# A transformer block with hedgehog linear attention: feature-map weights as one block spread by one-hot products, load waits as own queue entries, new orders of loads and queues

## The chip, the cores and the metric

The kernel runs on one core of one Trainium2 chip. The metric is the time of one execution in device microseconds (us). The profile is of one execution, taken by the hardware profiler.

## The reference, cut to what matters

One block on 2048 tokens of width 448, in bf16: a layer norm, linear attention with 16 heads of 28, a residual, a second layer norm, a gated unit of width 1792, a residual.

```
xn  = layernorm(x)
q, k, v = split(xn @ wqkv)                     # 16 heads, Dh = 28
pq, pk  = q @ w_phi[h], k @ w_phi[h]           # w_phi: 16 x 28 x 28
phi(p)  = concat(softmax(p), softmax(-p))      # 56 features
kv, z   = phi_k^T v, sum_s phi_k
o       = (phi_q kv) / (phi_q z + 1e-6)
h   = x + o @ wo
out = h + (sigmoid(n(h) @ w_gate) * (n(h) @ w_up)) @ w_down     # n = layernorm
```

## The kernel before, in words

Every piece of work is an entry (`op`, lines 29 to 67) with a name, an engine, a function and the keys that it reads and writes. `ORDER` (lines 221 to 288) writes out by hand, for each of the five engines, the names in the order in which its queue has them. `emit` (lines 110 to 191) works out from the keys which semaphores an entry waits for, issues the waits in front of it (lines 177 to 181), and leaves out those that the engine is already known to have passed. Queues are in order: an entry that waits holds up everything behind it on its engine. `PROGRAM` (lines 290 to 295) lists the stages of the second half.

The 2048 tokens are 16 tiles of 128. The names, with t for the tile:

- Loads, on SP's queue: x tiles (`x0`, `x1`, then two at a time as `x2`, `x4` and so on, line 480), `ld_k*` and `ld_v*` (the k and v thirds of wqkv), `ld_q*` (the q third, transposed by the DMA, line 483), `ld_wo*`, `ld_wg*`, `ld_wu*`, `ld_wd*`. `xT4` to `xT15`, `oT*` and `hT*` from tile 2 on are DMA transposes on the same queue (lines 563, 803, 839).
- First layer norm: `bst`/`agg` on DVE (lines 525, 526), `pow1_*` on POOL (534), `nm1_*` (538), `xn` (550 to 556, on ACT, DVE or POOL as `ORDER` says). For tiles 0 to 3 `xT` is a PE transpose (518) and `xTe` its copy out of PSUM (511).
- The feature map is folded into the weights. `Wphi` is a block-diagonal matrix for four groups of four heads: zeroed by `bd0` (line 415), then filled by four DMAs on ACT's queue, `wphi0` to `wphi3` (line 476), in rows of 56 bytes. `wT0` to `wT3` transpose Wk on PE (579), `wTe` copies the result out, `w2m0_*` multiplies it by Wphi (592) and `w2e0_*` copies that to SBUF as the folded k weights. `w2m1_*` and `w2e1_*` (592, 609) do the same for q, from the `ld_q` transposes.
- Projections: `ppa`/`ppb` and `vva`/`vvb` for tiles 0 to 3 in pairs, `pva`/`pvb` from tile 4 on (lines 628 to 639, products at line 309); the first need the folded k weights and xT, `vva0` the v weights. Per tile then: `ek` (two exponentials on ACT, 651 and 652), `v1` (v copied out, 511), `ss` and `rs` (sums and reciprocals on DVE, 655 and 661), `phi` (product on POOL or DVE, 665), and `kva`/`kvb`, which add the tile to kv in PSUM.
- q features: `pqa`/`pqb`, then `eq` on ACT (701). `kvz*` copy kv out by parts (730, 734), with `kvzones` (456), `mask2` (448) and `par` (450) as small constants made from the identity `ident` (417). `num`, `rsm`, `qq`, `b`, `c`, `rden` and `o` (lines 756 to 793) form the attention output.
- `woa`/`wob` are the output projection (848 to 872), `bs2`, `h`, `hn`, `hT` the residual, norm and transpose; `ga`/`gb` are gate and up (877 to 890), `sig` and `hh` the gate (891, 892), `dn`, `dp`, `dm`, `dl` the down products, `fin` the last residual (926), `out` the store.

At the start PE runs products of zeros (`warm0` to `warm9`, line 504) between its entries: 9 of 512 columns, then 35 of 128. Any PE entry that reads `wo` weights lists four load keys, any gate/up entry eight; the waits stand at the first such entry, `woa0` and `ga0_1`.

Of the kernel before, what the change touches and what calls it, by code (L numbers as in the profile page):

```python
# [6 lines left out]
ALU = mybir.AluOpType  # L7
# [11 lines left out]
class Graph:  # L19
# [90 lines left out]
    def emit(self, nc):  # L110
# [50 lines left out]
        with ExitStack() as es:  # L161
            sems = {n: es.enter_context(nc.semaphore("s_%s_%s" % n)) for n in names}
            with nc.Block() as block:
                start = {"sp": block.sync, "act": block.scalar, "pe": block.tensor, "dve": block.vector,
                         "pool": block.gpsimd}
                for e in ENGINES:
# [3 lines left out]
                    def body(eng, q=queues[e], e=e):  # L170
                        seen = {}
                        for n, o in enumerate(q):
                            if e == "sp" and n == len(q) - 5:
                                for sem, v in last_out.items():
                                    if sem[0] != "out":
                                        eng.wait_ge(sems[sem], v)
                            for j in o.waits:
                                p = ops[j]
                                if seen.get(p.sem, 0) < p.val:
                                    seen[p.sem] = p.val  # L180
                                    eng.wait_ge(sems[p.sem], p.val)
                            ins = o.fn(eng)
                            if o.dma is not None:
                                ins.then_inc(sems[o.sem], 16)
                            elif o.need_inc:
                                ins.then_inc(sems[o.sem], 1)
# [10 lines left out]
DH = 28  # L197
# [25 lines left out]
        "x1 x0 ld_k0 x2 ld_k2 x4 x6 ld_v0 x10 ld_v2 x8 ld_q2 ld_q1 ld_q0 x12 ld_q3 xT4 xT5 x14 xT6 xT7 xT8 xT9 xT10 "  # L223
# [6 lines left out]
        "wphi3 wphi2 wphi1 wphi0 par wTe0 xT0e nm1_3 w2e0_0 w2e0_2 w2e0_1 xT3e nm1_2 nm1_4 ek1 ek0 v1_1 v1_0 nm1_8 "  # L230
        "kvzones nm1_6 xn6 ek2 v1_2 ek3 v1_3 ek4 v1_4 w2e1_1 ek5 w2e1_0 ek6 v1_6 w2e1_3 ek7 v1_7 nm1_12 ek8 v1_8 "
        "w2e1_2 v1_9 ek9 ek10 v1_10 ek11 v1_11 v1_12 ek12 eq0_0p ek13 eq0_0m ek14 v1_14 ek15 v1_15 eq0_1p eq0_1m "
        "eq1_0m kvzC kvzA eq1_0p eq1_1p eq1_1m eq2_0p eq2_0m oT1e eq2_1p eq2_1m h0 h1 eq3_0m eq3_0p eq3_1p eq3_1m "
        "sig0_1 sig0_0 sig0_3 sig0_2 sig0_5 sig0_4 sq2 sig0_7 sig0_6 sq3 sig0_9 sig0_8 sig0_11 sig0_10 sig0_12 "
        "sig0_13 sq5 sq7 sq4 sig2_0 sig2_1 sq6 sig2_2 sig2_3 sig2_5 sig2_4 sig2_6 sig2_7 sig2_8 sig2_9 sig2_10 "
        "sig2_11 sig2_12 sig2_13 sig4_1 sq9 sig4_0 sig4_3 sq8 sig4_2 sig4_5 sig4_4 sig4_7 sig4_6 sig4_9 sq10 sig4_8 "
        "sq11 sig4_11 sig4_10 sig4_13 sig4_12 sig8_1 sig8_0 sq13 sig8_2 sig8_3 sig8_4 sig8_5 sq12 sig8_6 sq14 sq15 "
        "sig8_7 sig8_9 sig8_8 sig8_10 sig8_11 sig8_13 sig8_12 sig12_0 sig12_1 sig12_3 sig12_2 sig12_5 sig12_4 sig12_7 "
        "sig12_6 sig12_9 sig12_8 sig12_11 sig12_10 sig12_12 sig12_13 "
    ),  # L240
    "pe": (
        "warm0 warm1 warm2 xT1 warm3 wT0 warm4 wT1 warm5 warm6 xT0 warm7 wT2 w2m0_0 wT3 w2m0_2 w2m0_1 w2m0_3 warm8 "
        "warm9 xT3 ppa0 ppb0 vva0 xT2 vvb0 ppa2 vva2 ppb2 seed vvb2 w2m1_0 w2m1_1 pva4 kva0 pvb4 pva5 kvb0 kva1 pvb5 "
        "pva6 kvb1 pvb6 pva7 kva2 w2m1_3 w2m1_2 pvb7 pva8 kvb2 kva3 pvb8 kvb3 kva4 pva9 kvb4 pvb9 pva10 pqa0_0 pvb10 "
        "kva5 pva11 kvb5 kva6 pvb11 pva12 kvb6 kva7 pvb12 kvb7 pqb0_0 kva8 pva13 kvb8 kva9 pvb13 pva14 kvb9 kva10 "
        "pvb14 pva15 kvb10 kva11 pvb15 pqa0_1 kvb11 kva12 pqb0_1 pqa1_0 kvb12 kva13 pqb1_0 kvb13 kva14 kvb14 kva15 "
        "kvb15 qs pqa1_1 num0 pqb1_1 num1 pqa2_0 num2 pqb2_0 pqa2_1 oT0 oT1 num3 pqb2_1 woa0 wob0 num4 pqa3_0 pqb3_0 "
        "pqa3_1 num5 pqb3_1 hT0 hT1 num6 ga0_1 ga0_0 gb0_1 gb0_0 woa2 num7 ga0_3 ga0_2 gb0_3 gb0_2 wob2 num8 ga0_5 "
        "ga0_4 gb0_5 gb0_4 woa4 ga0_7 ga0_6 gb0_7 gb0_6 wob4 num9 ga0_9 ga0_8 gb0_9 gb0_8 woa6 ga0_11 ga0_10 gb0_11 "
        "gb0_10 wob6 ga0_13 ga0_12 gb0_13 gb0_12 dn0_0 dn0_4 ga2_1 ga2_0 gb2_1 gb2_0 num10 dn0_8 dn0_11 ga2_2 ga2_3 "  # L250
        "gb2_2 gb2_3 dp0_0 ga2_4 ga2_5 gb2_4 gb2_5 dp0_4 dp0_8 dp0_11 ga2_6 ga2_7 gb2_6 gb2_7 woa8 ga2_8 ga2_9 gb2_8 "
        "gb2_9 wob8 num11 ga2_10 ga2_11 gb2_10 gb2_11 dn2_0 ga2_12 ga2_13 gb2_12 gb2_13 dn2_4 dn2_8 ga4_1 num12 gb4_1 "
        "ga4_0 dn2_11 gb4_0 dp2_0 ga4_3 ga4_2 gb4_3 dp2_4 num13 gb4_2 ga4_5 dp2_8 gb4_5 ga4_4 dp2_11 gb4_4 ga4_7 "
        "num14 gb4_7 ga4_6 woa10 gb4_6 ga4_9 wob10 gb4_9 ga4_8 num15 gb4_8 ga4_11 woa12 gb4_11 ga4_10 wob12 gb4_10 "
        "ga4_13 dn4_0 ga4_12 gb4_13 gb4_12 dn4_4 ga8_1 ga8_0 gb8_1 gb8_0 dn4_8 dn4_11 ga8_3 ga8_2 dp4_0 gb8_2 dp4_4 "
        "dp4_8 gb8_3 ga8_4 dp4_11 gb8_4 ga8_5 woa14 gb8_5 ga8_6 wob14 gb8_6 ga8_7 dn6_0 gb8_7 dn6_4 ga8_8 ga8_9 dn6_8 "
        "gb8_9 gb8_8 dn10_0 dn6_11 ga8_11 ga8_10 gb8_11 gb8_10 dp6_0 dp6_4 dp6_8 ga8_13 ga8_12 gb8_13 gb8_12 dp6_11 "
        "dn10_4 dn10_8 ga12_0 ga12_1 gb12_0 dn8_0 dn10_11 gb12_1 ga12_2 dp10_0 ga12_3 dn8_4 dn8_8 gb12_3 gb12_2 "
        "dn8_11 dp10_4 ga12_5 dp8_0 ga12_4 gb12_5 gb12_4 dp8_4 dp8_8 ga12_7 ga12_6 gb12_7 gb12_6 dp10_8 dp10_11 "
        "dp8_11 ga12_9 ga12_8 gb12_9 gb12_8 dm14_0 dm14_4 dm13_0 dm14_8 dm12_0 dm13_4 ga12_11 ga12_10 gb12_11 gb12_10 "  # L260
        "dm15_0 dm15_4 dm13_8 ga12_12 ga12_13 gb12_12 gb12_13 dm14_10 dm12_4 dm13_10 dm12_8 dm13_12 dm13_13 dm12_10 "
        "dm14_12 dm12_12 dm12_13 dm15_8 dm14_13 dm15_10 dm15_12 dm15_13 dl15_0 dl15_12 "
    ),
    "dve": (
        "zero bd0 mask2 bst1 agg1 bst0 agg0 xn1 xT1e xn0 wTe1 bst3 bst2 agg3 wTe2 agg2 wTe3 bst4 w2e0_3 bst5 bst7 "
        "bst10 agg5 agg4 bst8 bst11 bst6 agg8 xT2e agg6 agg7 bst9 agg10 agg11 agg9 ss0 ss1 rs0 bst13 phi0 rs1 bst12 "
        "ss2 bst15 rs2 ss3 v1_5 bst14 ss4 agg14 rs3 rs4 agg13 agg12 phi3 agg15 ss5 ss6 rs5 rs6 phi5 ss7 rs7 phi6 ss8 "
        "rs8 xn14 ss9 ss10 rs9 rs10 phi9 ss11 rs11 v1_13 ss12 rs12 ss13 rs13 ss14 ss15 rs14 rs15 phi14 phi15 kvzD "
        "kvzB rsm0 qq0 b0 c0 b1 rden0 c1 rsm2 rden1 qq2 b2 c2 oT0e rsm3 qq3 b3 rden2 c3 o2 rden3 bs2_1 rsm4 bs2_0 qq4 "
        "ag2_1 ag2_0 b4 c4 hn1 hn0 rsm5 qq5 b5 hT0e c5 hT1e rden4 rsm6 rden5 qq6 b6 c6 hh0_1 rden6 hh0_0 rsm7 qq7 b7 "  # L270
        "c7 hh0_3 hh0_2 h3 h2 rden7 rsm8 qq8 hh0_5 hh0_4 b8 ve2 c8 hh0_7 hh0_6 h4 h5 hh0_9 hh0_8 hh0_11 hh0_10 h7 h6 "
        "rsm9 hh0_12 hh0_13 qq9 b9 ve5 c9 ve7 hh2_0 rden8 rsm10 hh2_1 qq10 ve6 o8 b10 hh2_2 nm4 hh2_3 rden9 nm5 o9 "
        "c10 hh2_4 hh2_5 fin1 fin0 hh2_6 hh2_7 hh2_8 hh2_9 h9 h8 hn7 rden10 hh2_10 hh2_11 rsm11 qq11 nm9 b11 hh2_13 "
        "c11 hh2_12 rsm12 qq12 nm8 b12 c12 rden11 hh4_1 hh4_0 o10 hh4_3 rsm13 qq13 b13 rden12 hh4_2 c13 hh4_5 fin3 "
        "hn9 rden13 hh4_4 hn8 fin2 rsm14 hh4_7 o13 qq14 b14 c14 hh4_6 h10 h11 nm10 hh4_9 nm11 rsm15 hn10 hh4_8 hn11 "
        "hh4_11 qq15 h13 h12 hh4_10 b15 c15 hh4_13 nm13 hh4_12 nm12 rden15 o15 rden14 hh8_1 hh8_0 o14 hh8_2 hh8_3 "
        "fin4 fin5 hh8_4 hh8_5 h15 h14 nm14 hh8_6 nm15 hn12 hn14 hh8_7 hh8_9 hh8_8 hn13 hn15 hh8_11 hh8_10 hh8_12 "
        "hh8_13 fin6 fin7 hh12_0 hh12_1 hh12_3 hh12_2 hh12_5 hh12_4 hh12_7 hh12_6 fin9 fin11 fin10 fin8 hh12_9 hh12_8 "
        "hh12_10 hh12_11 hh12_12 hh12_13 fin13 fin12 fin14 fin15 fin15b "
    ),  # L280
    "pool": (
        "v1ones neghalf ident0 ident phipad opad0 wqpad steps pow1_1 pow1_0 pow1_3 xn3 pow1_2 xn2 epsl0 pow1_4 xn4 "
        "xn5 epsr0 pow1_6 nb1_6 pow1_8 xn7 xn8 phi1 xn9 phi2 xn11 xn10 phi4 pow1_12 xn12 xn13 phi7 phi8 xn15 phi10 "
        "phi11 phi12 phi13 o0 o1 o3 pow2_1 pow2_0 o4 o5 o6 nm3 o7 pow2_2 ve3 nm2 hn2 pow2_3 hn3 nm6 nm7 ve4 pow2_5 "
        "pow2_4 pow2_6 hn4 pow2_7 hn6 hn5 ve8 ve9 o11 pow2_9 o12 pow2_8 ve10 pow2_10 ve11 pow2_11 ve12 pow2_12 ve14 "
# [40 lines left out]
def build(nc, A_x, A_wqkv, A_w_phi, A_wo, B_w_gate, B_w_up, B_w_down, out):  # L326
# [10 lines left out]
    with ExitStack() as es:  # L337
# [31 lines left out]
        Wphi = sb("Wphi", [GP, G, GP])  # L369
        wo_e = sb("wo_e", [P, KT, D])  # L370
# [44 lines left out]
        op("dve", "bd0", lambda e: e.memset(Wphi[:], 0.0), w=["Wphi"])  # L415
# [59 lines left out]
        for hl in range(4):  # L475
            load("wphi%d" % hl, Wphi[hl * DH:(hl + 1) * DH, :, hl * DH:(hl + 1) * DH],
# [521 lines left out]
```

## Time and profile before

| | |
|---|---|
| median of 3 runs | 204.35 us (203.64 to 205.31) |
| the profiled execution | 203.49 us, of which the span of its instructions is 201.6 |
| busy in the span | PE 195.6, DVE 132.4, ACT 91.6, POOL 58.1 us |
| first projection (`ppa0`) starts | 9.98 us |
| `pva4` starts | 17.63 us |
| `num0` starts | 45.37 us |
| `ga0_1` starts | 59.19 us |
| last product ends, last residual starts | 199.27 us, 199.30 us |

All times in the views are from the start of the span. In a timeline a row has the start, the time to the end of the merged instructions, the engine, the line, operation, tiles and count, and in brackets the engine's idle time before and what ended it. PEld is PE's load of weights, a "q" behind an engine its sequencer. A granted clock of 1.00 is full speed.

### The profile page before, as it was taken

The numbers are of one execution on the slowest core, as the hardware profiler recorded it, in microseconds if no ns is written. First come the engines' busy times: TensorE is split into PE (matmuls) and PEld (weight loads), VectorE is DVE, ScalarE is ACT, GpSimd is POOL, SyncE is SP. The second block draws the span as 40 slices with busy tenths as digits, with TensorE's granted clock in tenths as the row PEclk, the third lists the DMA queues.
The fourth block names the chain that finished last, engine by engine and source line by source line (L and its number), as shares of the span: only waits on it lengthen the run. The fifth ranks groups of instructions, "written<-read, shape, count | busy, mean of one in ns | idle before, by whom it ended". The sixth has DMA issues, their size and how long they took to land.

```text
span 201.6 us, 5872 instructions
## 1 busy us (share of the span) xinstructions
PE 195.6 (97%) x2508; PEld 112.1 (56%) x2508; DVE 132.4 (66%) x319; ACT 91.6 (45%) x191; POOL 58.1 (29%) x94
## 2 busy tenths in 40 slices
PE   7999999999979999999999999999999999999995
PEld 2935555666558768676444444555555555544443
DVE  5899999778999858757758877436432422272224
ACT  2678988999672637222333442324322212222220
POOL 6489998823333534600041110001400000000000
PEclk9999999999999999999999999999999999999999
DMA  6965642679983240241005411030222000004003
GB/s 155 313 142 130 65 70 55 178 246 271 298 201 77 43 57 3 54 79 29 0 3 124 81 27 25 7 71 24 57 50 52 0 3 0 0 3 137 0 0 94
DMA packets 32867, 16.27 MB, mean 81 GB/s; under 512 B 25096, under 2 KB 31944, under 8 KB 32840
## 3 DMA queue, kind: packets, MB, share of 16 engines
q1 hardware_dynamic: 32336, 15.86, 33.9%
q8 instruction: 20, 0.33, 0.7%
q10 hardware_dynamic: 504, 0.03, 0.2%
q14 instruction: 7, 0.06, 0.1%
HBM read 8.34 MB, written 1.84 MB: 50 GB/s over the span
## 4 chain that ended last, share of the span: by engine, by line
PE 88%; DVE 4%; ACT 3%; POOL 3%; issue 1%; POOLq 0%
PE psum L309 79%; PE psum L919 5%; PE psum L504 2%; ACT eq L701 1%; POOL xn_pad L556 1%; POOL rst L534 1%; PE psum L592 1%; PE psum L518 1%; ACT kvz L734 1%; DVE st L809 1%; DVE xnT L511 1%; POOL rst L813 1%; DVE st L525 1%; ACT xn_pad L550 0%; DVE hn_pad L831 0%
## 5 line engine op out<-in xcount | busy, mean ns | idle before, releaser
L309 PE MATMUL psum<-xnT,wg_sb 64*128 64x512 bf16 (+1 forms) x490 | 93.1, 333 | 0.3 <-DVE rden L786 0.2
L309 PE MATMUL psum<-xnT,wu_sb 64*128 64x512 bf16 (+1 forms) x490 | 92.9, 333 | 0.0
L891 ACT ACTIVATE sg_sb<-psum 128x512 bf16<-128x512 f32 (+1 forms) x70 | 34.8, 512 | 91.4 <-PE psum L309 90.9
L892 DVE SCALAR_TENSOR_TENSOR hhT<-sg_sb,psum 128x512 bf16<-128x512 bf16 (+1 forms) x70 | 38.9, 576 | 54.4 <-ACT sg_sb L891 54.1
L309 PEld LDWEIGHTS psum<-xnT,wg_sb 64*128 64x128 bf16 x490 | 44.3, 94 | 22.6 <-DVE hhT L892 4.2
L309 PEld LDWEIGHTS psum<-xnT,wu_sb 64*128 64x128 bf16 x490 | 44.3, 94 | 13.1
L309 PE MATMUL psum<-wd_sb,hhT 64*128 64x448 bf16 x336 | 36.9, 349 | 0.0
L309 PEld LDWEIGHTS psum<-wd_sb,hhT 64*128 64x128 bf16 x336 | 17.5, 94 | 14.6 <-DVE x_sb L816 0.5
L309 PE MATMUL psum<-Wk,xnT 64*128 64x448 bf16 x112 | 22.1, 350 | 0.7 <-ACT v L511 0.3
L309 PE MATMUL psum<-wv_sb,xnT 64*128 64x448 bf16 x112 | 22.4, 351 | 0.0
L825 POOL TENSOR_SCALAR ve<-ssq 128x1 f32<-128x1 f32 x10 | 2.0, 203 | 55.5 <-ACT junk L822 55.2
L655 DVE TENSOR_REDUCE ss<-hhT 128x32 f32<-128x896 bf16 x16 | 16.6, 1060 | 0.0
L665 POOL TENSOR_TENSOR phi<-hhT,rs 128x896 bf16<-128x896 bf16 x9 | 15.6, 1745 | 1.7 <-DVE rs L661 0.8
L701 ACT ACTIVATE eq<-psum 120x1024 bf16<-120x1024 f32 x16 | 15.5, 1030 | 1.2 <-PE psum L309 1.1
L309 PE MATMUL psum<-xnT,Wq 64*120 64x512 bf16 x112 | 14.8, 383 | 0.1
L309 PE MATMUL psum<-wo_o,oT 64*128 64x448 bf16 x56 | 13.2, 349 | 0.0
L309 PE MATMUL psum<-wo_e,oT 64*128 64x448 bf16 x56 | 13.2, 349 | 0.0
L790 POOL TENSOR_TENSOR o_pad<-c_sb,rden 128x448 bf16<-128x448 bf16 x9 | 8.3, 937 | 14.3 <-DVE rden L786 14.2
L309 PEld LDWEIGHTS psum<-Wk,xnT 64*128 64x128 bf16 x112 | 7.8, 94 | 6.7 <-issue 1.1
L926 DVE SCALAR_TENSOR_TENSOR x_sb<-psum,x_sb 128x448 bf16<-128x448 f32 (+2 forms) x17 | 9.4, 592 | 2.7 <-PE psum L919 1.6
L919 PE MATMUL psum<-wd_sb,hhT 128*128 128x448 bf16 (+2 forms) x70 | 11.1, 316 | 0.0
L781 DVE TENSOR_TENSOR b_sb<-psum,qq 128x464 bf16<-128x464 f32 x16 | 10.2, 637 | 0.7 <-PE psum L309 0.5
(100 smaller groups left out, 235.0 us busy)
## 6 DMA issues: line engine op xcount, KB each, us to landing
out_dram<-x_sb SPq DMA_DIRECT2D x15, 112.0 KB, 1.8
x_sb<-in_A_x_dram SPq DMA_DIRECT2D x7, 224.0 KB, 4.7
wd_sb<-in_B_w_down_dram SPq DMA_DIRECT2D x7, 224.0 KB, 5.1
wg_sb<-in_B_w_gate_dram SPq DMA_DIRECT2D x3, 448.0 KB, 6.1
wu_sb<-in_B_w_up_dram SPq DMA_DIRECT2D x3, 448.0 KB, 5.5
wv_sb<-in_A_wqkv_dram SPq DMA_DIRECT2D x2, 224.0 KB, 5.1
wk_sb<-in_A_wqkv_dram SPq DMA_DIRECT2D x2, 196.0 KB, 3.5
wo_e<-in_A_wo_dram SPq DMA_DIRECT2D x1, 336.0 KB, 4.4
```

Source lines behind the costliest of these rows:

```text
L309: p = e.matmul(o, lhsT=w, rhs=r, start=st, stop=sp, tile_position=(row, 0))
L504: p = e.matmul(bk(3)[:, 0:size], lhsT=zero[:, 0:P], rhs=zero[:, 0:size], start=True, stop=True)
L511: op(("act", "dve"), name, (lambda e: e.copy(dst, src), lambda e: e.tensor_copy(dst, src)), r=[rkey], w=[wkey])
L655: op("dve", "ss%d" % t, lambda e: e.tensor_reduce(ss[:, s, :].rearrange("p (b h) -> p b h", h=2), eks.rearrange("p b (d h) -> p b h d", h= ...
L665: return e.tensor_tensor(phi[:, sp, :, :, :].rearrange("p b a n -> p (b a) n")[:, :, 0:56].rearrange("p b (d h) -> p b d h", h=2), eks.rea ...
L701: op("act", "eq%d_%d%s" % (c, i, "pm"[sg]), lambda e, sg=sg: e.activation(eq[c][:, sg, 2 * i:2 * i + 2, :].rearrange("p g n -> p (g n)"), ...
L781: op("dve", "b%d" % t, lambda e: e.tensor_tensor(h3(b_sb), OMv[:, :, :, 0:EV], h2(qq)[:, :, :, None].to_broadcast([P, NB, 8, EV]), ALU.mul ...
L790: return e.tensor_tensor(o_pad[:, t % NO, off:off + D].rearrange("p (h d) -> p h d", h=H), c_sb[:, t % NS, :, 0:DH], rden[:, t % NS, :][:, ...
L891: op("act", "sig" + nm, lambda e: e.activation(sg_sb[:, k, 0:N], bk(bg)[:, 0:N], ACT.Tanh, scale=0.5), r=[B(bg)], w=[("sg", k)])
L892: op("dve", "hh" + nm, lambda e: e.scalar_tensor_tensor(out=hhT[(t0 // 4) % NHH][:, ff, ns], in0=sg_sb[:, k, 0:N], scalar=1.0, in1=bk(bu)[ ...
L919: p = e.matmul(bk(b)[:, lo:hi], lhsT=hb[:, ff, TS(t)], rhs=wd_sb[:, ff, lo:hi], start=ff == 0, stop=ff == FT - 1)
L926: op("dve", "fin%d%s" % (t, nm), lambda e: e.scalar_tensor_tensor(out=h_sb[:, t, lo:hi], in0=bk(b)[:, lo:hi], scalar=0.5, in1=h_sb[:, t, l ...
```

## The change

- The four DMAs into Wphi and its memset are gone. One DMA on ACT's queue brings the 16 x 28 x 28 weights as one flat block into `wph`, 112 rows of 112 numbers (224 bytes): row r holds four pieces of 28 numbers, pieces 4r to 4r + 3 of the 448 rows `28 h + i` (head h, input row i). `zsel` is a one-hot matrix of 112 x 452, made by one POOL select. Sixteen products of 28 columns (`wsp`, on PE) with windows of `zsel` as weights spread the pieces, so that PSUM has for each of the 112 rows of a group the 28 numbers of that row's head. One multiply on DVE (`wex`), by `hmask` (one-hot of the head in its group, a reduction of the identity), writes the block-diagonal Wphi.
- Two entries without an instruction of their own, `wwo` and `wgu`, carry the waits for the wo loads and for the gate and up loads on PE; they stand behind `kva14` and behind `pqb3_0`.
- The warm-up is 6 products of 512 columns and 30 of 128.
- All five queues have new orders in the first 70 us or so. On SP `ld_k2` is ahead of `x2`, `x8` ahead of `x6`, `ld_v0` behind `x6`, `ld_q2` and `ld_q1`, `x12` and `x14` behind `xT4`. To other engines go `wTe2`, `wTe3`, `v1_5` (from DVE to ACT), `par` (ACT to DVE), `xn6` (ACT to POOL), `xn1` (DVE to POOL), `xn2`, `xn11`, `xn12` (POOL to DVE), `phi1`, `phi11`, `phi12` (POOL to DVE), `phi0`, `phi9` (DVE to POOL), `o2` and `ve2` (DVE to POOL), `nm1_2` is no longer needed and `nm1_1` is, `nb1_6` is no longer needed. `oT0e`/`oT1e` and `kvzB`/`kvzC` swap between ACT and DVE.

```diff
-        "x1 x0 ld_k0 x2 ld_k2 x4 x6 ld_v0 x10 ld_v2 x8 ld_q2 ld_q1 ld_q0 x12 ld_q3 xT4 xT5 x14 xT6 xT7 xT8 xT9 xT10 "
+        "x1 x0 ld_k0 ld_k2 x2 x4 ld_v2 x8 x6 ld_q2 ld_q1 ld_v0 x10 ld_q0 ld_q3 xT4 x12 x14 xT5 xT6 xT7 xT8 xT9 xT10 "
...
-        "wphi3 wphi2 wphi1 wphi0 par wTe0 xT0e nm1_3 w2e0_0 w2e0_2 w2e0_1 xT3e nm1_2 nm1_4 ek1 ek0 v1_1 v1_0 nm1_8 "
-        "kvzones nm1_6 xn6 ek2 v1_2 ek3 v1_3 ek4 v1_4 w2e1_1 ek5 w2e1_0 ek6 v1_6 w2e1_3 ek7 v1_7 nm1_12 ek8 v1_8 "
+        "wphi kvzones nm1_1 wTe0 wTe2 wTe3 w2e0_0 nm1_3 w2e0_2 w2e0_1 xT0e xT3e ek0 ek1 v1_0 nm1_6 v1_1 ek3 ek2 v1_2 "
+        "v1_3 w2e1_1 nm1_8 w2e1_0 ek4 v1_4 w2e1_2 ek5 v1_5 w2e1_3 v1_6 ek6 nm1_12 v1_7 ek7 ek8 v1_8 eq0_0p ek9 v1_9 "
...
-        "warm0 warm1 warm2 xT1 warm3 wT0 warm4 wT1 warm5 warm6 xT0 warm7 wT2 w2m0_0 wT3 w2m0_2 w2m0_1 w2m0_3 warm8 "
-        "warm9 xT3 ppa0 ppb0 vva0 xT2 vvb0 ppa2 vva2 ppb2 seed vvb2 w2m1_0 w2m1_1 pva4 kva0 pvb4 pva5 kvb0 kva1 pvb5 "
+        "warm0 warm1 warm2 wsp warm3 wT0 wT1 warm4 wT2 wT3 warm5 w2m0_0 w2m0_1 w2m0_2 warm6 w2m0_3 xT1 xT0 warm7 "
+        "warm8 warm9 xT3 ppa0 ppb0 xT2 vva0 seed vvb0 ppa2 ppb2 vva2 vvb2 kva0 w2m1_1 w2m1_0 kvb0 pva4 kva1 pvb4 pva5 "
...
-        "zero bd0 mask2 bst1 agg1 bst0 agg0 xn1 xT1e xn0 wTe1 bst3 bst2 agg3 wTe2 agg2 wTe3 bst4 w2e0_3 bst5 bst7 "
+        "zero hmask mask2 bst1 bst0 agg1 agg0 wex wTe1 bst3 bst2 agg3 xn0 agg2 bst4 xT1e w2e0_3 agg4 bst5 xn2 agg5 "
...
-        "v1ones neghalf ident0 ident phipad opad0 wqpad steps pow1_1 pow1_0 pow1_3 xn3 pow1_2 xn2 epsl0 pow1_4 xn4 "
+        "phipad opad0 neghalf ident0 ident zsel steps epsl0 v1ones pow1_1 pow1_0 xn1 pow1_3 xn3 pow1_2 nm1_4 pow1_4 "
...
-        op("dve", "bd0", lambda e: e.memset(Wphi[:], 0.0), w=["Wphi"])
+        op("pool", "zsel", lambda e: e.affine_select(out=zsel[:], in_=zero[:GP, 0:452], compare_op=ALU.not_equal, fill=1.0,
+                                                     base=3, pattern=[[-1, 452]], channel_multiplier=4),
+           r=["zero"], w=["zsel"])
...
-        for hl in range(4):
-            load("wphi%d" % hl, Wphi[hl * DH:(hl + 1) * DH, :, hl * DH:(hl + 1) * DH],
-                 A_w_phi.rearrange("(g hl) i j -> hl i g j", hl=4)[hl], [("Wphi", hl)], 6, r=["Wphi"], eng="act")
+        load("wphi", wph[:], A_w_phi.rearrange("h i j -> (h i j)").rearrange("(r c) -> r c", c=GP), ["wph"], 25, eng="act")
+        op("dve", "hmask", lambda e: e.tensor_reduce(hmask[:], ident[:GP, 0:GP].rearrange("p (l i) -> p l i", i=DH), AX.X, ALU.add),
+           r=["ident"], w=["hmask"])
+
+        def spread(e):
+            for gg in range(G):
+                for m in range(4):
+                    z = GP * gg - m + 3
+                    p = e.matmul(bk(2)[:GP, gg * DH:(gg + 1) * DH], lhsT=zsel[:, z:z + GP], rhs=wph[:, m * DH:(m + 1) * DH],
+                                 start=m == 0, stop=m == 3)
+            return p
+        op("pe", "wsp", spread, r=["zsel", "wph"], w=[B(2)])
+        op("dve", "wex", lambda e: e.tensor_tensor(Wphi[:].rearrange("p g (l f) -> p g l f", f=DH),
+                                                   bk(2)[:GP, 0:GP].rearrange("p (g f) -> p g f", f=DH)[:, :, None, :].to_broadcast([GP, G, 4, DH]),
+                                                   hmask[:, None, :, None].to_broadcast([GP, G, 4, DH]), ALU.mult),
+           r=[B(2), "hmask"], w=["Wphi"])
...
-        for i, (n, size) in enumerate(((9, 512), (1, 128), (1, 128), (2, 128), (1, 128), (8, 128), (4, 128), (7, 128), (9, 128), (2, 128))):
+        for i, (n, size) in enumerate(((4, 512), (2, 512), (1, 128), (2, 128), (1, 128), (6, 128), (4, 128), (6, 128), (8, 128), (2, 128))):
...
+        for n, keys in (("wwo", wo_keys), ("wgu", wgu_keys)):
+            op("pe", n, lambda e: None, r=keys, rows=64)
```

## The prediction

> **What bounds the kernel now.** I read the page's parts 1 to 3 first, then a table of busy time by stage, then the timelines of the engines in the first 60 us, the only stretch that the diff rewrites in depth.
>
> ```profile
> PE 195.6 (97%) x2508; PEld 112.1 (56%) x2508; DVE 132.4 (66%) x319; ACT 91.6 (45%) x191; POOL 58.1 (29%) x94
> PE   7999999999979999999999999999999999999995
> DVE  5899999778999858757758877436432422272224
> q10 hardware_dynamic: 504, 0.03, 0.2%
> ```
>
> TensorE is busy 97% of the span, but VectorE too is full in slices 2 to 12. The stages (columns: stretch, its length, then busy PE, PEld, DVE, ACT, POOL with counts, granted clock, DMA share, GB/s):
>
> ```profile
> 9.98:17.63 7.65, 7.07 (x71) 3.20 (x71) 7.65 (x22) 6.16 (x17) 6.38 (x13) 1.00 0.60 120
> 17.63:43.16 25.53, 25.41 (x450) 15.09 (x450) 24.18 (x45) 22.94 (x51) 22.30 (x17) 1.00 0.58 124
> 45.37:59.19 13.82, 12.55 (x209) 7.12 (x209) 12.80 (x37) 11.67 (x14) 3.93 (x6) 1.00 1.01 262
> 59.19:199.27 140.08, 139.92 (x1628) 79.53 (x1628) 79.28 (x194) 44.11 (x99) 20.43 (x39) 1.00 0.18 40
> ```
>
> From 59.19 to 199.27 PE idles 0.16 us in 140: nothing can be gained there, and whatever the first 59 us gain or lose arrives at the end one for one. From 17.63 to 43.16 PE has 0.12 us idle, DVE only 1.35. The first projection starts at 9.98 and ends the prologue:
>
> ```profile
> 1.18 4.24 PE L504 MATMUL psum<-zero 128*128 128x512 bf16 x11 [1.18 <-DVE zero L414]
> 8.05 1.78 ACT L511 CAST Wk<-psum 128x448 bf16<-128x448 f32 x3
> 9.05 0.66 DVE L511 CAST Wk<-psum 128x448 bf16<-128x448 f32 x1
> 9.98 1.73 PE L309 MATMUL psum<-Wk,xnT 64*128 64x448 bf16 x14
> ```
>
> It waits for the third of ACT's copies of the folded k weights (9.83), not for the feature-map weights: the fold's first product ran at 7.58, right behind other PE work. Later come a PE wait on ACT, DVE's last slack and its last phi, and two starts of PE that only its own issuing delays:
>
> ```profile
> 17.63 0.35 PE L309 MATMUL psum<-Wk,xnT 64*128 64x448 bf16 x1 [0.33 <-ACT v L511]
> 36.22 0.63 DVE L511 CAST v<-psum 128x448 bf16<-128x448 f32 x1 [1.02 <-PE psum L309]
> 41.88 1.14 DVE L665 TENSOR_TENSOR phi<-hhT,rs 128x896 bf16<-128x896 bf16 x2
> 51.06 0.13 PEld L309 LDWEIGHTS psum<-x_sb,ident 64*128 64x128 bf16 x2 [0.24 <-issue]
> 59.16 0.09 PEld L309 LDWEIGHTS psum<-xnT,wg_sb 64*128 64x128 bf16 x1 [0.28 <-issue]
> ```
>
> **The change, part by part.** The profiled execution took 203.49 us (span 201.6, 1.9 around it); the median of the three runs is 204.35, 0.86 above. I sum against 203.49 and add 0.86 at the end.
>
> *Weights as one block.* Gone: four ACT issues (1.93 us from 1.39, before ACT's table load), 504 small packets (0.2% of 201.6 us on all engines, 0.4 us of load stream in the first 6 us), the memset of Wphi (0.24, DVE). New: one ACT issue (about 0.42), which nothing waits for; a POOL select over 452 columns (row L417: 0.29 for 128; between 0.29 and, scaled, 1.04; I take 0.7, as most of POOL's rows grow with width); hmask on DVE (0.29, row L448); 16 products; one DVE multiply (0.64, row L781, same kind and size from PSUM). POOL reaches ident at about 2.1 instead of 1.51, since phipad and opad0 go ahead, so the select ends near 3.1; PE is in its warm-up until 1.18 + 6 x 0.43 = 3.75 and hides it. The 16 products cost 0.055 each at the later pace (L504, 11 in 0.78) or 0.107 at the early one (128 columns of the 0.43 per 512): 0.9 to 1.7 us. They run before PE's doubling near 5.1, so I take 1.5: end at 5.3, multiply done near 6.1. Wphi is thus no earlier than now.
>
> *To the first projection.* DVE's bst3, bst2 and xn0 queue behind the multiply, so xn0 ends near 7.9 (now 6.46); ACT takes wTe2 and wTe3 (0.53 each), then w2e0_0, nm1_3, w2e0_2, w2e0_1 and xT0e. ACT from wT0's end, about 5.8: 3 x 0.48 + 3 x 0.62 + 0.1 + 0.6, with short waits for nm1_3 and the fold = 9.6 to 9.85, against 9.83 for the last weight copy now. Bounds for this term: -0.6 (no waits, and 0.4 of load stream lands usefully) and +0.8 (products at the slow pace, all of xn0's lateness shown). I take -0.15; it is nearest to ACT's row.
>
> *Projections up to 17.63.* PE's own work there is 4 x 1.31 + 0.2 + 0.1 + 0.4 = 5.95 of 7.65. ACT loses xn6 (0.81) with its 0.55 wait for nb1_6; kvzones (0.30) moves into its idle start. But bank 0 must still wait for ek2 and v1_2 after ek3, so pva4 starts at about 17.5 by ACT's rows (ek 0.97, v1 0.54); what is gained is that kva0 and kvb0 (0.2 each) run before it. PE: -0.15 - 0.4 = -0.55 here.
>
> *Loads on SP.* ld_k2 passes x2; x2 lands later, about 6.5, when DVE asks for it at 6.4. ld_v0 falls behind x6 and two ld_q transposes (1.47 + 1.25 of issue): issued near 7.75, landing 2.9 (x12's row) to 5.3 us (wv_sb) later, 10.65 to 13.0; vva0 wants it at 11.4. In order of bytes it lands near 11.1: cost 0, bounds 0 and +1.0. x12 and x14 go behind xT4, which waits for xn4: x12 lands near 17.5, bst12 wants it at 17.6; cost 0, bound +0.6 on DVE. xT5 moves behind both issues (1.2 us) and is wanted only at 19. ld_q0 and ld_q3 gain or lose under 1 us and are wanted at 16.7.
>
> *The balance of the kv stage.* From the first projection to phi15 DVE gains xn2, xn11, xn12 (0.33 each), phi1, phi11, phi12 (0.53 each) and par (0.15), and loses phi0, phi9 (0.53 each) and v1_5 (0.54): +1.15 us. POOL loses about 1.9 and is no bound. DVE's slack is the 1.02 at 36.22 plus 0.4 between phi15's end (43.02) and the product that needs it (43.39). So DVE allows at most 1.02 + 0.4 + 0.15 - 1.15 = 0.4 us of PE's 0.55. I carry **-0.3** past kvb15; bounds -0.6 and +1.7 (all of the extra DVE work and 0.5 of late start shown).
>
> *Weight waits of their own.* wwo waits behind kva14, where kvb14 has to wait for kva14's end anyway (PE gaps 0.06 at 43.16); the wo loads are issued no later than now and land by about 41.7. wgu waits behind pqb3_0, near 55; the last wu load is there about 54.4, and PE's next stall (0.95 at 58.59, on c_sb) would absorb a late one. woa0 and ga0_1 then start without their 4 and 8 load waits: of 0.18 us (oT1e ends 50.94, start 51.12) and 0.15 to 0.32 (59.04 or 58.87 to 59.19), two thirds at most. I take **-0.1** and **-0.15**; bounds 0 and -0.35 together.
>
> *Rest.* o2 and ve2 go to POOL, which idles there (3.9 of 13.8 busy); DVE's 0.5 us stands before a wait for PE (53.26) and buys nothing. num9's new place and the swapped gate steps of tiles 0 and 1 leave PE's work the same in a stretch with no idle.
>
> Sum: -0.3 - 0.1 - 0.15 = **-0.55**: 202.95 on the profiled basis, 203.8 against the median.
>
> **The rivals.**
>
> *DVE binds the kv stage (slower).* Place: phi1 to phi15 between 17 and 43 us. For it: 24.18 of 25.53 busy, +1.15 of new work. Against it: 1.4 of slack. It decides once the slack lost to waits (for the multiply, x12, ek) passes 0.3 us; price +0.3 to +1.7, less 0.25 from the waits: 204.4 to 205.8, typically 205.0.
>
> *The clock doubles later (slower).* Warm-up products of 512 columns fall from 9 to 6, and sixteen 28-column products take their place when the pace has not doubled (until 4.99 the trace starts a 512 each 0.43 us; from 5.46 a 128 each 0.055). If the array counts these as idle, wT, xT and fold products (40 x 0.055) run at half pace: 2.2 us more on PE, of which the evacuations hide about half: +1.1, or 204.9; if it lasts to the end of the first two projections (7 pairs of 0.19 us at full pace), they take +1.3 more, 206.2. It decides from about 7 us on, when the fold starts. The Trainium skill's "TensorE: Matmul & The Clock Gate", Part 1, says that the clock doubles after some 3.4 us of sustained activity in a free-running window, and that transposes do not count as busy in the same way: by that rule the sum would be 204.9 rather than 202.95 + 0.86, if the thin products reset the window. This trace agrees on the delay (1.18 to 5.1, 3.9 us), but its pace had doubled before the transposes became the main work, so it cannot show what thin products do.
>
> *The head gain goes through whole (faster).* If DVE keeps its early idle and the x loads land 0.4 us sooner, all of 0.4 + 0.55 and 0.35 of waits arrive: -1.3, 203.05. All of PE's idle from 9.98 to 59.19 (0.58 + 0.12 + 0.21 + 1.27) would be -2.2, 202.15; the drain between paired products makes that unlikely.
>
> *The block does nothing and ld_v0 is late.* Wphi is not what PE waits for now; a landing at 12.4 instead of 11.1 puts +0.7 on vva0; with no gain but the 0.25 of the waits: 204.8.
>
> **How the numbers follow.** Forecast 0.45 (203.2 to 204.4 by its own bounds); DVE binds 0.22; clock 0.11; ld_v0 0.07; head gain whole 0.15. A measurement of this kernel can tell about 1% (2 us) from no change: below 202.3 is faster, above 206.4 slower. Faster takes 0.08 from the last case and 0.05 from the forecast with the runs' own spread (203.64 to 205.31); slower takes 0.05 from the clock and 0.09 from DVE binding, at its upper end or with that spread. The range 202.2 to 206.0 leaves out the tails of both.
>
> **What would show it.** Right: ppa0 near 9.8; kva0 before pva4, at 17.5; DVE without gaps until phi15 near 42.7; num0 near 45.1; woa0 within 0.1 us of its transpose copy; ga0_1 near 58.65; from there 140.1 us as now. Wrong: 128-column products still 0.107 apart after 5.5; vva0 waiting for wv_sb; PE waiting for DVE phi between 18 and 43; or ga0_1 later than 59.2.

## The result, and the profile after

The changed kernel takes 205.33 us in the median of 12 runs (203.78 to 205.87); the kernel before, in 12 runs beside it, 203.86 us (203.16 to 205.31). The ratio is 1.0057, 95% interval 1.0036 to 1.0079: slower by about 1.2 us (the medians differ by 1.47). The forecast was 0.55 us faster. The time lies in the forecast range only because the range was wide; the direction was wrong.

The times of the changed kernel are not spread evenly. With the later runs there are 25 of it: 8 from 203.52 to 203.97, 17 from 204.99 to 205.87, none between. The kernel before has no such gap. No disturbance of the chip makes the two groups: they come from this kernel's start, as the experiments show. I call them the early and the late group, since what parts them is when TensorE doubles its pace.

The profiled execution took 203.93 us (span 202.0), so it belongs to the early group. It is 0.44 us slower than the profiled execution of the kernel before, but the early group as a whole (median 203.84) is level with the median of that kernel: the larger part of the loss is in the late group. Of the page, parts 1 and 4:

```profile
PE 196.1 (97%) x2516; PEld 113.1 (56%) x2516; DVE 132.2 (65%) x319; ACT 92.7 (46%) x191; POOL 56.4 (28%) x95
...
PE 91%; DVE 4%; DMA 2%; SPq 1%; issue 1%; POOL 1%
```

The stages, with the same columns as before:

```profile
10.00:17.63 7.63, 7.43 (x82) 3.24 (x79) 7.54 (x22) 5.55 (x13) 6.32 (x12) 1.00 0.62 159
17.63:43.16 25.53, 25.46 (x434) 15.45 (x434) 24.93 (x48) 22.91 (x51) 18.55 (x15) 1.00 0.53 121
59.19:199.27 140.08, 139.92 (x1642) 79.77 (x1635) 79.46 (x195) 44.53 (x99) 20.59 (x40) 1.00 0.18 41
```

PE is as dense in the kv stage as it was (25.46 of 25.53) and DVE carries 0.75 us more there. In the chain that ended last, 2% is now a load of x: the wait for x2 in the head, below. The head and four later points, from timelines of the same execution:

```profile
3.81 1.10 PE L490 MATMUL psum<-wph,zsel 112*112 112x28 bf16 x16
5.07 0.62 PE L599 MATMUL psum<-ident,wk_sb 112*112 112x112 bf16 x8
...
6.68 1.15 DVE L545 BATCH_NORM_STATS2 st<-x_sb 128x6 f32<-128x448 bf16 x2 [0.56 <-DMA x_sb<-in_A_x_dram]
...
9.79 0.38 PE L538 MATMUL psum<-ident,xn_pad 128*128 128x128 bf16 x4 [0.23 <-DVE Wk L531]
10.11 0.55 PE L311 MATMUL psum<-Wk,xnT 64*128 64x448 bf16 x4
...
18.00 0.35 PE L311 MATMUL psum<-Wk,xnT 64*128 64x448 bf16 x1
...
45.80 0.39 PE L311 MATMUL psum<-kvz,eq 56*128 56x60 bf16 x15
...
59.41 0.09 PEld L311 LDWEIGHTS psum<-xnT,wg_sb 64*128 64x128 bf16 x1
```

Against before: `ppa0` 10.11 (9.98), `pva4` 18.00 (17.63, but now with `kva0` and `kvb0` done), `num0` 45.80 (45.37), `ga0_1` 59.45 (59.19; its first weight load, in the last row, starts without the 0.28 us of issue that it had). The last product ends 0.34 us later. From `ppa0` to `kvb15` it is 34.00 us against 33.66.

The sixteen spreading products took 1.10 us because the pace doubled among them, at 4.1 us; the execution profiled of the kernel before doubled at 5.4. This moment is read from the starts of equal products; the page shows the granted clock as full from the first slice on. The record of the clock in the trace agrees with the products: its first entry, at full clock, begins at 4.11 us in this execution and at 5.37 in that of the kernel before, and the page counts the time ahead of the first entry as full.

### The profile page after: what moved, and what is told of

It reads as the page before. It is cut to its first block, busy times and chain, and to the rows that moved or that the text cites. A ratio compares the mean times of both kernels' runs of the same rounds, so it can differ in the third digit from the quotient of the medians.

```text
span 202.0 us, 5885 instructions
## 1 busy us (share of the span) xinstructions
PE 196.1 (97%) x2516; PEld 113.1 (56%) x2516; DVE 132.2 (65%) x319; ACT 92.7 (46%) x191; POOL 56.4 (28%) x95
## 4 chain that ended last, share of the span: by engine, by line
PE 91%; DVE 4%; DMA 2%; SPq 1%; issue 1%; POOL 1%
PE psum L311 84%; PE psum L941 5%; DMA x_sb<-in_A_x_dram 2%; SPq L415 1%; DVE st L545 1%; PE psum L538 1%; DVE st L829 1%; POOL rst L833 1%; PE psum L612 0%; DVE hn_pad L851 0%; DVE xnT L531 0%; DVE b_sb L801 0%; DVE Wk L531 0%; DVE c_sb L804 0%; DVE rsm L798 0%
## 5 line engine op out<-in xcount | busy, mean ns | idle before, releaser
L685 POOL TENSOR_TENSOR phi<-hhT,rs 128x896 bf16<-128x896 bf16 x8 | 13.6, 1711 | 6.2 <-DVE rs L681 3.8
L810 POOL TENSOR_TENSOR o_pad<-c_sb,rden 128x448 bf16<-128x448 bf16 x10 | 9.3, 935 | 14.9 <-DVE rden L806 14.8
L941 PE MATMUL psum<-wd_sb,hhT 128*128 128x448 bf16 (+2 forms) x70 | 11.1, 315 | 0.0
```

The lines of the kernel that those rows point to most:

```text
L685: return e.tensor_tensor(phi[:, sp, :, :, :].rearrange("p b a n -> p (b a) n")[:, :, 0:56].rearrange("p b (d h) -> p b d h", h=2), eks.rea ...
L810: return e.tensor_tensor(o_pad[:, t % NO, off:off + D].rearrange("p (h d) -> p h d", h=H), c_sb[:, t % NS, :, 0:DH], rden[:, t % NS, :][:, ...
L941: p = e.matmul(bk(b)[:, lo:hi], lhsT=hb[:, ff, TS(t)], rhs=wd_sb[:, ff, lo:hi], start=ff == 0, stop=ff == FT - 1)
```

## The experiments

Theory 1: TensorE doubles its pace at a moment that wanders from execution to execution, and the new head makes it miss that moment in most of them. Theory 2: a load lands late. Theory 3: the new order of the kv products costs 0.3 us. The kernel before, run beside the experiments three times, took 203.75, 203.85 and 203.64 us. "Early" and "late" are counts of runs of the two groups.

**The changed kernel again, twice.** No edit.

> The changed kernel as it is, once more. Its runs so far fall into two groups, near 203.9 and 205.0 to 205.9, and the profile showed the quick one. Theory 1 (clock): the slow group is a late doubling of TensorE's pace, since only 6 products of 512 columns now stand before thin products and waits; a profile of a slow execution would show 128-column products still 0.107 us apart beyond 6 us and ppa0 near 11.3 instead of 10.1. Theory 2 (loads): x2 or a later load lands up to 1.5 us later; ppa0 late with DVE idle before bst3, or a wait of PE for a load later on. Theory 3 (placement of kv products): the loss stands between 10 and 44 us in every execution and there is no second group. Time 203.8 to 205.9 in any case.

Measured: 205.09 us (203.52 to 205.69), ratio 1.0046 (1.0016 to 1.0076), 5 early, 7 late; profiled at 203.96, early, with the pace doubling at 4.7.

> The changed kernel once more, one look, to see a slow execution (two of three are). If it is one (205.0 to 205.9), theory 1 asks that the pace doubles between 8.5 and 10.8 us, that the moment 3.4 us before it has the spreading products behind it, and that ppa0 starts near 11.4; the rest of the trace should be the quick one's, shifted. A doubling near 4 to 5 us in a slow run would refute it.

Measured: 205.16 us, a late one. PE's timeline of this execution:

```profile
3.81 1.63 PE L490 MATMUL psum<-wph,zsel 112*112 112x28 bf16 x16
5.29 0.37 PE L524 MATMUL psum<-zero 128*128 128x128 bf16 x2
5.46 0.95 PE L599 MATMUL psum<-ident,wk_sb 112*112 112x112 bf16 x8
6.20 0.31 PE L524 MATMUL psum<-zero 128*128 128x128 bf16 x1
6.31 0.95 PE L599 MATMUL psum<-ident,wk_sb 112*112 112x112 bf16 x8
...
7.70 1.33 PE L612 MATMUL psum<-Wphi,WkT 112*128 112x112 bf16 x12
8.81 0.52 PE L524 MATMUL psum<-zero 128*128 128x128 bf16 x4
9.17 0.36 PE L612 MATMUL psum<-Wphi,WkT 112*128 112x112 bf16 x4
...
11.42 0.74 PE L311 MATMUL psum<-Wk,xnT 64*128 64x448 bf16 x6
```

Eight transposes take 0.95 us here and 0.62 in the early execution, twelve fold products 1.33 and not 0.81: the pace doubles only at 9.1. There is no stall on a load: PE has work without a gap from 3.81 to 9.4, at half pace. `ppa0` starts at 11.42, 1.31 later than in the early execution, and from there all is the same: `ga0_1` is 1.30 later (60.75), the time 1.23. Theory 2 falls as the cause of the late group, which is this difference.

**Nine products of 512 columns.**

```diff
-((4, 512), (2, 512), (1, 128), ...
+((4, 512), (5, 512), (1, 128), ...
```

> The changed kernel with 9 instead of 6 products of 512 columns at the start, as before the change. Theory 1 (clock): the pace has doubled before the thin products in every execution; runs near 203.9, 1.2 to 1.5 us below the changed kernel's median. Theory 2 (loads) and theory 3 (kv placement): no change, as PE waits there for x2 anyway; if the feature-map weights then become the last thing that the fold waits for, at most +0.4.

Measured: 204.39 us, ratio to before 1.0055 (1.0025 to 1.0086): 8 runs from 203.92 to 204.49, 4 from 206.08 to 206.42. The late group got rarer and longer, and did not go. The simple form of theory 1, too few wide products, was wrong. In the profile the spreading products run from 5.09 and the pace doubles at 6.2 with twelve of them done.

**The suspect alone: thin or wide products of zeros in the kernel before.** In place of three of the nine products of 512 columns:

```diff
+            if i == 0:
+                def thin(e):
+                    for _ in range(16):
+                        p = e.matmul(bk(3)[:GP, 0:28], lhsT=zero[:GP, 0:GP], rhs=zero[:GP, 0:28], start=True, stop=True)
```

with 112 for 28 in the second kernel.

> The kernel before with 3 of its 9 warm-up products of 512 columns replaced by 16 products of zeros of 28 columns (the shape of the spreading products, same place in time, nothing else of the change). Theory 1, as the traces now put it: in six profiles the pace doubled at 4.1, 4.7, 4.9, 5.4, 6.2 and 7.2 us, so the moment wanders from one execution to the next over some 3.4 us; thin products keep TensorE occupied (0.094 us each) but stream only 28 columns, and a moment that has all of them behind it is missed, so that the pace doubles 3.4 us later. Then about two runs of three lie 1.2 to 2.0 us above the others, median near 205.2. Rival (loads or orders make the slow group): no second group, 203.4 to 204.6 like the kernel before; +0.2 at most.

> As the run beside it, but the 16 products of zeros have 112 columns and not 28: the same number of products, the same place and at the slow pace nearly the same time. Theory 1: no second group, 203.0 to 204.6, median within 0.3 of the kernel before. Rival (fewer products of 512 columns is enough): two groups as in the run beside it. Both wrong if this one is slower by itself.

Measured: thin 205.18 us, five runs from 203.18 to 204.35 and seven from 205.07 to 206.78, ratio 1.0028 (0.9993 to 1.0063, without the two longest runs); wide 204.17 us (203.00 to 205.18), ratio 1.0011 (0.9983 to 1.0039), spread like the kernel before. Above 205.0 lie seven of twelve thin runs, two of twelve wide ones and one of 35 of the kernel before. The two differ in nothing but the columns that a product streams. Their timelines, thin first:

```profile
3.71 1.63 PE L513 MATMUL psum<-zero 112*112 112x28 bf16 x16
...
5.99 0.58 PE L586 MATMUL psum<-ident,wk_sb 112*112 112x112 bf16 x4
...
8.52 0.55 PE L505 MATMUL psum<-zero 128*128 128x128 bf16 x7
```

```profile
3.71 1.70 PE L513 MATMUL psum<-zero 112*112 112x112 bf16 x16
...
6.04 0.37 PE L586 MATMUL psum<-ident,wk_sb 112*112 112x112 bf16 x4
```

At the half pace sixteen products take about the same time, 1.63 and 1.70 us; the count and the occupied time are equal. The profiled thin one (205.07) doubled at 8.5, the wide one (203.93) at 6.0. So thin products can make the doubling late in a kernel that has nothing else of the change; the counts alone (seven against two of twelve) would be weak evidence.

**The spreading products behind the transposes.** Nine products of 512 columns, `wsp` behind `wT3`, `wex` behind `bst2`.

> The changed kernel with 9 products of 512 columns first and the spreading products moved behind the transposes of the k weights (the multiply behind bst2 on DVE): until about 6.5 us TensorE sees only wide products. Theory 1: the slow group is gone, all runs between 203.6 and 205.0; the fold is later by about 1.2 us, which costs 0 to +0.6 of ppa0 in a quick execution: median near 204.2. Rival (loads or orders): the slow group stays, 205 to 206.5 in two runs of three.

Measured: 205.05 us (204.76 to 205.38), ratio 1.0048 (1.0026 to 1.0071). One group, the narrowest of all, as theory 1 has it; the profiled execution doubled at 5.7, ahead of the spreading products. But the late fold cost more than the 0 to 0.6 us that I wrote: the multiply starts at 7.48, the first fold product at 8.14 (6.58 in the early execution), `ppa0` at 11.22.

**Orders without the block.** The changed kernel's five orders, with the old memset, the four DMAs and nine products of 512 columns.

> The changed kernel's orders, waits and load order, but the feature-map weights come as before (memset, four DMAs, no spreading products) with 9 products of 512 columns. It parts the two halves of the change. Theory 1: one group; what is left is the kv stage's loss (0.34 us from ppa0 to kvb15) and the late x2, less 0.17 at ga0_1: +0.2 to +0.5 against the kernel before, median near 204.2. Rival (the orders make the slow group): two groups, median near 205.

Measured: 204.26 us (203.82 to 205.03), ratio 1.0022 (0.9999 to 1.0046), one group. `ppa0` to `kvb15` takes 34.00 us as in the changed kernel. The orders don't make the late group. What they cost is not shown by the times: the medians differ by 0.4 us, but the interval reaches below 1, and the next kernel, which has the same orders, measured 1.0005.

**The spreading products made wide.** The same sixteen products read their 28 columns four times over:

```diff
-rhs=wph[:, m * DH:(m + 1) * DH],
+rhs=wph[:, None, m * DH:(m + 1) * DH].to_broadcast([GP, 4, DH]),
```

> The changed kernel with one thing altered: the sixteen spreading products read their 28 columns four times over (112 columns, written as four copies), and the multiply reads the copies instead of one copy four times. Same count, same place, same result. Theory 1 (thin products make the doubling be missed): the slow group is gone, runs between 203.5 and 205.0, median 204.2 (0.9 below the changed kernel), +0.3 against the kernel before from the kv stage. Rival (something else in the changed head makes it): the slow group stays in about two runs of three, median 205.1.

Measured: 203.96 us (203.40 to 204.26), ratio 1.0005 (0.9985 to 1.0026): the late group is gone, and 1.1 us with it. From the timeline:

```profile
3.81 1.70 PE L490 MATMUL psum<-wph,zsel 112*112 112x112 bf16 x16
...
5.53 0.95 PE L600 MATMUL psum<-ident,wk_sb 112*112 112x112 bf16 x8
...
6.38 0.60 PE L600 MATMUL psum<-ident,wk_sb 112*112 112x112 bf16 x8
```

The profiled execution doubled at 6.4, between the two groups of transposes and with all the sixteen products behind it (3.81 to 5.5). In no profiled execution did it double with the sixteen thin ones just behind it. None of twelve runs is late, where 17 of 25 were: this settles theory 1 within the changed kernel. The transposes stand in the same place in both kernels, so it is not they that make the late group.

**x2 ahead of the second k load**, in the kernel with wide products.

> The run beside it with x2 ahead of ld_k2 on SP, as before the change. The late x2 (0.56 us of idle DVE in the profile, in the chain that ended last) is the next suspect: bst3 0.5 us sooner, ppa0 0.2 to 0.5 sooner, median 203.8 to 204.0. Rival: the k weights are then what waits (wT2 0.4 later), no change or +0.2.

Measured: 204.23 us (203.61 to 204.82), ratio 1.0023 (1.0003 to 1.0042). No gain: the k weights then come late (PE stands 0.52 us ahead of `wT2`). This does not show that the 0.56 us that DVE waits for x2 in the early execution of the changed kernel costs nothing: in the profiled execution with wide products DVE did not wait for x2 at all (`bst3` starts at 6.82, without idle time before it), so in that execution there was nothing to gain.

**Two kv products between `pva` and `pvb`.** In the changed kernel six `kvb` go from before a `pva` to behind it.

```diff
...
-kvb7 pva13 kva8 pvb13 kvb8 pva14 kva9 pvb14
+pva13 kvb7 kva8 pvb13 pva14 kvb8 kva9 pvb14
...
```

> The changed kernel with six kvb products moved behind the following pva, so that between pva and pvb stand two kv products and not one (as before the change). Theory 3 (kv placement): a lone kv product costs 0.19 to 0.24 us, as it uncovers PE's drain, a pair 0.23 together; six lone ones less: -0.5 to -0.9 between pva4 and num0, if DVE keeps up. Rival: DVE binds there, then no change (within 0.15), and PE waits for phi in place of its own drain. Theories 1 and 2: no change.

Measured: 205.92 us (205.53 to 207.74, 6 runs), ratio 1.0119 (1.0085 to 1.0154): by the medians slower by another 0.8. Like against like it is more: the profiled execution (205.53) doubled at 4.9, so it is an early one, and lies 1.6 above the early ones of the changed kernel; from `ppa0` to `kvb15` it takes 36.06 us against 34.00. Theory 3 in this form is wrong as a cure. The waits of PE between 17 and 46 us:

```profile
PE psum L312 <- ACT v L532: 0.8, 2, 0.5
PE psum L312 <- ACT hhT L673: 0.3, 1, 0.3
PE psum L312 <- issue: 0.2, 1, 0.2
```

The changed kernel has only one row there, 0.2 us. The moved `kvb` had stood between `pvb` and the next `pva` (0.58 and 0.19 us from start to start); without it that `pva` starts 0.77 us after `pvb` all the same, so the move gains nothing there, and PE waits for ACT's copies besides. What makes up the rest of the 2.06 us stays open.

The head of this kernel is that of the changed one, and its early execution shows something else:

```profile
6.14 1.14 DVE L546 BATCH_NORM_STATS2 st<-x_sb 128x6 f32<-128x448 bf16 x2
...
9.57 1.74 PE L312 MATMUL psum<-Wk,xnT 64*128 64x448 bf16 x14
```

Here x2 was there in time, and `bst3` starts at 6.14 without a wait. In the two early executions of the changed kernel it starts at 6.68 and 6.91, behind waits of 0.56 and 0.62 us for x2. In all three `ppa0` starts 3.43 us after `bst3` (9.57, 10.11, 10.34), whether the pace doubled at 4.9, 4.1 or 4.7. So in these three it is `bst3`, held up by x2 in two of them, and not the moment of the doubling, that sets `ppa0`.

**The weight waits alone**, in the kernel before.

> The kernel before with only the two entries for the weight waits (wwo, wgu). By the two traces: ga0_1 0.17 us sooner behind num6, woa0 no sooner; -0.15 against the kernel before. Rival: nothing (the wait at ga0_1 is the transposes' copies, not the load waits), 0.0. It should show none of the changed kernel's loss and no second group.

Measured: 204.01 us (202.96 to 204.62), ratio 1.0000 (0.9978 to 1.0023). From `num6` to `ga0_1` it is 0.42 us against 0.60, as in the changed kernel; 0.18 us is less than the runs can tell. In this execution the pace doubled at 7.2, and `ppa0` was at 10.81 against 9.98 with a doubling at 5.4: the kernel before wanders too, but without a gap in its times.

**Block and waits in the old orders** (wide products, six of 512 columns).

> The kernel before with the flat block (wide spreading products, 6 products of 512 columns ahead of them) and the two weight-wait entries, all other orders as before. What the two sound parts of the change are worth by themselves: no slow group; -0.17 at ga0_1; the 504 small packets and ACT's three issues gone, but the multiply's 0.6 us on DVE before xT1e: -0.3 to +0.3 in the head. Median 203.4 to 204.0 against 203.85. If the loads land sooner for the block, ppa0 falls below 9.9 for the same moment of doubling.

Measured: 204.25 us (203.90 to 205.12), ratio 1.0032 (1.0013 to 1.0052), one group, no gain. The multiply (5.44, 0.62 us) stands ahead of `xT1e` on DVE, which starts at 6.08 instead of 5.71; `ppa0` is at 10.53 for a doubling at 6.3, where the kernel with wide zeros had 10.40 for 6.0. No kernel here beats the one before beyond what its runs can tell.

## Why the prediction was wrong, point by point

**Weights as one block: the step that failed.** Its small prices held: the select took 0.56 us and ended at 2.66 (0.7 and 3.1 forecast), sixteen products 1.1 to 1.6 us (1.5), and the multiply ended at 5.57 or 6.1 (6.1). But the step says "They run before PE's doubling near 5.1, so I take 1.5". It took the doubling, seen in one execution, for a fixed point that the products could not move. (In that execution it lies at 5.4: products of 128 columns start 0.107 us apart up to 5.3. The delay from PE's first product at 1.18 is 4.2 us and not 3.9.) It is not fixed (4.1 to 7.2 us in twelve profiles, none of which had all sixteen thin products just behind it), and the products do move it (8.5 and 9.1 in the other two). The term for them was 1.5 us, hidden; what they cost is a whole later doubling, 1.3 us at the first projection in two runs of three.

**To the first projection: -0.15 forecast.** +0.13 in the early execution, +1.44 in the late one (11.42 against 9.98). Here the whole miss of the late group lies. In the early execution the last wait ahead of `ppa0` is not for ACT, whose row the forecast followed, but for DVE's copy of the folded weights (9.06 to 9.71, the row at 9.79 above), and DVE had waited for x2. With x2 in time, in the kernel with the pairs, `ppa0` came 0.41 before that of the kernel before.

**The rival that came true** is "the clock doubles later", given 0.11 and 204.9 us. Its mechanism and its place were right, and its size was near: the late group's lower edge is 204.99, its middle 205.4. I gave it too little since I asked only whether thin products put off the doubling in the execution shown. With a moment that falls anywhere, it was a question of shares. The step between moments can be read from the traces: where the record of the clock was kept, the full clock lasts 197.97 us in nine executions and 194.56 in the two late ones, 58 and 57 times 3.413 us. An estimate from this step and from the earliest moment seen, 4.1: the moments lie between 4.1 and 7.5, and those from about 5.1 on have all the thin products behind them, 2.4 of 3.4, or 0.7, against 17 of 25 counted. With nine products of 512 columns the thin ones end 1.3 us later, the estimated share falls to about a third, and 4 of 12 were counted.

The Trainium skill says the same of the step: "TensorE: Matmul & The Clock Gate", Part 1, has the doubling after a window of 3413 ns in a free-running count. These runs agree, by the 197.97 and 194.56 us, and also in that 3.4 us before the late doublings at 8.5 and 9.1 lie 5.1 and 5.7, where the thin products had just been. The same part of the Trainium skill says that the warm-up is an amount of time and not a number of products; here sixteen products that occupied the same time did or did not count by their width, which it does not say. It has the moment vary by 0.5 us either way; here it lies anywhere from 4.1 to 7.2. The words on transposes that the prediction puts under Part 1 of that page of the Trainium skill stand in its Part 4; the run with wide products, whose transposes are the same, shows that they do not make the late group.

**Projections up to 17.63: -0.55 forecast with the head.** `pva4` came 0.37 later, with 0.36 us of kv products (0.24 and 0.12 by the rows of before) done ahead of it: in like terms nothing gained or lost, 0.13 made up since `ppa0`.

**Loads on SP: right for two, wrong for x2.** ld_v0 landed at 11.06 (11.1 forecast) and `vva0` did not wait; x12 landed at 16.85, in time. x2 was put at 6.5, when DVE would ask for it at 6.4, and priced at nothing. In the early execution DVE was free at 6.1 and waited 0.56, and `ppa0` came 0.54 later than with x2 in time (10.11 against 9.57).

**The balance of the kv stage: wrong sign, and not by the rival's reason.** -0.3 was carried past kvb15; it is +0.47. DVE never became the bound: it has gaps of 0.38 and 0.22 us and `phi15` ends at 43.31, ahead of its product. PE's own order costs more. Two kv entries in a row, in the timeline of before, and one alone, in that of after:

```profile
30.98 0.39 PE L309 MATMUL psum<-v,phi 64*128 64x58 bf16 x16
31.21 0.36 PE L309 MATMUL psum<-wv_sb,xnT 64*128 64x448 bf16 x1
```

```profile
31.88 0.29 PE L311 MATMUL psum<-v,phi 64*128 64x58 bf16 x8
32.12 0.36 PE L311 MATMUL psum<-wv_sb,xnT 64*128 64x448 bf16 x1
```

From the start of the kv products to that of `pvb` it is 0.23 us for sixteen products and 0.24 for eight: the second entry was free. Summed from start to next start between `ppa0` and `kvb15`, the 31 kv entries take 4.50 us before and 5.42 after; the other entries give 0.58 back. I had looked at the engines' sums, in which both kernels are equally dense, and not at what stands between two products. The pairing experiment shows that the lone entries also hide something, so this is an account of the 0.34 us in the traces, not a cure, and its cause is not shown.

**Weight waits: half right.** woa0 gained nothing (5.75 us after `num0` in both), ga0_1 0.18 (0.15 forecast). **Rest: right**, 140.1 us from `ga0_1` on in both.

Together: 0.43 later at `num0`, less 0.17 at `ga0_1`, is what the early execution loses by then; 1.3 more from the doubling, in two runs of three, is the rest. These terms set one execution of each kernel side by side, with doublings at 4.1 and 5.4.

## What to carry to other kernels

In a warm-up it counts how wide the products are, not only that PE is occupied: sixteen products of 28 columns made PE miss the doubling, sixteen of 112 did not. So count the columns that PE streams in the 3.4 us before any moment at which it could double, and widen thin products where width is free; here they started 0.094 us apart at the half pace with 28 columns and 0.093 with 112. Look at the list of times before reading the one profile: two groups mean that the profile shows only one of them. And where an edit touches the start, treat the doubling as a moment that can fall anywhere (4.1 to 7.2 us here), and price each share of it.

## What the runs showed of the hardware

A product of 112 rows and 28 columns takes 0.094 us at the half pace and 0.052 at the full one, as much as one of 112 columns (0.093 and 0.052), so the wide spreading products cost no time. A doubling came with twelve thin products (1.1 us) just behind it, at 6.2; all sixteen (1.5 us) were too many. Where between them the limit lies was not tried, nor what transposes count for. The profile's granted clock reads 1.00 through the slow stretch too, so that the pace has to be read from the products themselves.
